# Three chained layers on one core: every low plane of the expert weights on VectorE, none on GpSimd

## The chip, the core and the metric

The kernel runs as one program on one core of a Trainium2 chip. A core has TensorE for matrix products, VectorE, ScalarE and GpSimd for work on tiles in on-chip memory, and SyncE, whose queue here issues most of the DMA transfers. In the profile these are PE (with PEld for the loading of weights), DVE, ACT, POOL and SP. The metric is the device time of one execution in microseconds (us). A difference is given against the kernel before.

## What is computed

Causal attention feeds a mixture of eight experts, in which every token goes to one expert, and that feeds a dense layer with `h - tanh(h)` between its two products. All inputs and outputs are float32.

```python
# attention: batch 4, 12 heads, 448 tokens, head size 64
scores = q @ k.T / 8, causal mask, softmax;  attn_out = attn @ v
x = attn_out as (1792, 768)
# experts: w1 is (8, 768, 1024), w2 is (8, 1024, 768)
logits = x @ w_gate;  e_idx = argmax(logits)
for e in range(8):
    mask = e_idx == e
    h = maximum(x[mask] @ w1[e], 0)
    out[mask] = gate_w * sigmoid(x @ w_output_gate)[e] * (h @ w2[e])
# dense layer: w_in is (768, 2048), w_out is (2048, 768)
h = x @ w_in;  return (h - tanh(h)) @ w_out
```

## The kernel before

Matrix products run in 16 bits. To keep accuracy, each operand is split into two float16 planes: a **high plane**, the value scaled by `WS` and rounded, and a **low plane**, the scaled value minus the high plane. A product takes three passes: high by high, high by low and low by high.

The program has three stages. In the expert stage the tokens of one expert are worked on in **slots** of 128. `slot()` first multiplies with w1 in two halves (72 matmuls each, tile `ph`); after each half `slot_relu` makes the high plane `hh` on ScalarE and the low plane `hl` on VectorE. Then it multiplies with w2 (tile `py`) in two column halves; each reads `hh` and `hl` block by block, the first four blocks from the first half of w1's product, the last four from the second. In between, TensorE transposes the rows of the next slot, and ScalarE and VectorE copy these out (tiles `xT`, `xT_n`, line 150 and 152). Every expert runs its first slot always, and further ones (`extra`, line 871) only if it has enough tokens: a branch on a count, which every engine takes for itself. With the data of the runs, experts 0, 3 and 5 run no further slot, experts 1, 4 and 7 run one, expert 2 two and expert 6 four. Expert 0's first slot in this stage is its second 128 tokens. The further slots also convert pieces of the dense layer's weights (`conv`: tiles `cu`, `cc`, `co`, stored to `wb_d`).

In the first slot of expert e the weights of expert e+1 are split. A **piece** is one block of 128 rows of w1 (128x1024, six of them) or of w2 (128x768, eight of them). `PLAN` lists the pieces in four groups. Each entry says which weight, which block, which engine makes the high plane (`scaled`, lines 112, 114 or 116), and which the low one (`rest_of`, line 120 on VectorE, lines 114 and 128 on GpSimd, where it takes a scaling into the scratch tile `scm` and a subtraction, in parts of 512 columns at most). Group by group, `fill_hi` and `fill_lo` are called at fixed places in `slot()`: the low planes of group 0 stand on their engine's queue between the two `hl` of the slot, those of groups 1 and 2 among the copies of transposed rows, those of group 3 at the end. After the low planes of a group, SyncE issues the loads of the same blocks of expert e+2 (`load_raw`, line 104): each waits until the piece in `raw1` or `raw2` has been read. Behind the last of them SyncE stores the slot's result (line 857), and then comes the branch at line 871. With expert 1, VectorE also makes the tables for the tokens' order (`order_a`, lines 1031 and 1039) ahead of group 3, and TensorE multiplies them (tile `order`, line 1058) before expert 1's further slot.

GpSimd's own queue also issues the gathers of token rows (`slot_rows`, line 801), which stay.

Of the kernel before, what the change touches and what calls it, by code (L numbers as in the profile page):

```python
# [26 lines left out]
E, F1 = 8, 1024  # L27
# [29 lines left out]
def build(ctx: ExitStack, tc: tile.TileContext, kq0, kq, v, wg, wo, w1, w2, wf, out):  # L57
# [45 lines left out]
    def load_raw(e, x, k, n=1):  # L103
        nc.sync.dma_start(out=(raw1, raw2)[x][:, k : k + n, :], in_=(w1, w2)[x][e, :, k : k + n, :])

    def w_tiles(e, zs=(0, 1)):
        return [w16s[e % 2][z].tile((([128, 2, KD, F1]), [128, 2, KF1, DM])[z], F16, tag=f"w{z + 1}", name=f"w{z + 1}_{e}")
                for z in zs]
# [9 lines left out]
    def rest_of(eng, out, in_, hi):  # L118
        if eng == "v":
            nc.vector.scalar_tensor_tensor(out=out, in0=in_, scalar=WS, in1=hi, op0=ALU.mult, op1=ALU.subtract)  # L120
        else:
            w = in_.shape[-1]
            h = scr[0].shape[-1]
            for o in range(0, w, h):
                c = slice(o, min(o + h, w))
                t = scr[0][:, 0 : c.stop - o]
                scaled("p", t, in_[:, c])
                nc.gpsimd.tensor_tensor(out=out[:, c], in0=t, in1=hi[:, c], op=ALU.subtract)  # L128

    def pieces_hi(w, plan):  # L130
        for x, k, eh, el in plan:
            scaled(eh, w[x][:, 0, k, :], (raw1, raw2)[x][:, k, :])

    def pieces(w, plan, nxt=None, hi=True):
        if hi:
            pieces_hi(w, plan)
        for x, k, eh, el in plan:
            rest_of(el, w[x][:, 1, k, :], (raw1, raw2)[x][:, k, :], w[x][:, 0, k, :])
        if nxt is not None and nxt < E:
            for x, k, eh, el in plan:  # L140
                load_raw(nxt, x, k)
# [751 lines left out]
    def conv_load(dst, r, eng=nc.sync):  # L893
        eng.dma_start(out=dst.rearrange("p n t -> p (n t)").unsqueeze(1), in_=wf32[:, ds(r, 1), :])
# [15 lines left out]
    def conv_fill(e, i):  # L910
# [4 lines left out]
        def fill(z):  # L915
# [10 lines left out]
    wi = [t.rearrange("p a b -> p (a b)").bitcast(F16).rearrange("p (c k f) -> p c k f", c=4, k=KD)  # L926
          for t in (raw1, raw2)]
    wif = [t.rearrange("p c k f -> p (c k f)") for t in wi]
    PLANS = {0: [[(1, 2 * z, "a", "p"), (1, 2 * z + 1, "a", "v")] for z in range(4)],
# [4 lines left out]
    PLAN = (  # L934
# [4 lines left out]
    )  # L939
    tpool = [mp_t]  # L940
    first = {}
    NI = 12
# [16 lines left out]
    def prep0(g, i, r0=None):  # L959
        bk = GS[g] + i  # L960
        src = ys_d[bk * 128 : (bk + 1) * 128] if r0 is None else ys_d[ds(r0, 128)]
        nc.sync.dma_start(out=yg_of(g, i), in_=src)
# [67 lines left out]
    def order_a(z):  # L1030
        eq = lambda t, pos, h, n: nc.vector.tensor_tensor(
            out=t, in0=pos.unsqueeze(2).to_broadcast([CP, h, n]), in1=io[:CP, 0:n].unsqueeze(1).to_broadcast([CP, h, n]),
            op=ALU.is_equal)
        if z < 2:
            cs = slice(z * NC_ // 2, (z + 1) * NC_ // 2)
            eq(oba[:, cs], pb[:, 0, cs], NC_ // 2, 128)
        else:
            eq(obm, pb[:, 1], NC_, NBLK)
            nc.vector.tensor_tensor(out=obb, in0=obm.unsqueeze(3).to_broadcast([CP, NC_, NBLK, 5]),
                                    in1=pcs.unsqueeze(2).to_broadcast([CP, NC_, NBLK, 5]), op=ALU.mult)  # L1040
# [23 lines left out]
    wts = {0: wts0, 1: wts1 + w_tiles(1, (1,))}  # L1064
# [14 lines left out]
    for e in range(E):  # L1079
# [7 lines left out]
        if e + 1 < E:  # L1087
            if e:
                wts[e + 1] = w_tiles(e + 1)

            def fill_hi(z, e=e):
                plan = PLANS.get(e, PLAN)
                todo = (plan[0][:2], plan[0][2:])[z] if z < 2 else plan[z - 1]
                pieces_hi(wts[e + 1], todo)

            def fill_lo(z, e=e):
                if e == 0 and z >= 2:
                    next(tl, None)
                pieces(wts[e + 1], PLANS.get(e, PLAN)[z], e + 2, False)
                if e == 1 and z > 1:  # L1100
                    order_a(z) if z < 3 else order_b()

            fill = (fill_hi, fill_lo)
        else:
            wo_ = [w16s[0][z].tile([128, KF2, DM], F16, tag=tg, name=f"wo_{z}") for z, tg in enumerate(("w1", "w2"))]
            wof = [t.rearrange("p k f -> p (k f)") for t in wo_]
            stg = [wof[0][:, z * 4096 : (z + 1) * 4096].bitcast(U32).rearrange("p (n t) -> p n t", t=2) for z in range(2)]
            stg += [wof[1][:, z * 2048 : (z + 1) * 2048] for z in range(2)]
            tot = nc.values_load(flg[0:1, 1:2], min_val=0, max_val=3 * MAXI)
            remaining(NDY - 2)  # L1110
            first["yg"] = [wof[1][:, z * 2 * DM : (z + 1) * 2 * DM].bitcast(F32) for z in range(3)]
            at_ = (wof[1][:, 6 * DM :], wof[0])
            first["yq"] = [[t[:, z * 2 * DM : (z + 1) * 2 * DM].rearrange("p (k x n) -> p k x n", k=KD, x=2)
                            for z in range(3)] for t in at_]
            first["dg"] = [[t[:, 6 * DM + 256 * z : 6 * DM + 256 * (z + 1)].bitcast(BF16).rearrange(
                "p (a n) -> p a n", a=2) for z in range(3)] for t in at_]
            first["sc"] = [t[:, 6 * DM + 768 : 6 * DM + 832].bitcast(F32) for t in at_]
            second = nc.values_load(flg[0:1, 0:1], engines=(SP,), min_val=0, max_val=128)
            for i in range(GB[0]):
                prep0(0, i, second * i if i else 0)  # L1120

            def fill(z):
                if z == 2:
                    for q in range(2):
                        conv_load(stg[q], NDY + q, nc.gpsimd)
                if z in (1, 2):
                    conv(cu[z - 1], co[z - 1][:, 0], co[z - 1][:, 1], "p")
                    conv_store(z - 1, nc.values_load(flg[0:1, z + 1 : z + 2], engines=(SP,), min_val=0, max_val=NDY - 1))
                if z == 3:
                    first_prep()  # L1130
# [241 lines left out]
```

## Time and profile before

| | before |
|---|---|
| time of three runs | 1077.86 us median (1073.29 to 1078.04) |
| the profiled execution: its time, its span | 1075.26 us, 1073.5 us |
| TensorE's granted clock, mean | 0.986 of full speed |
| attention stage | 0 to about 260 us |
| expert stage, experts 0 to 6 whose first slots split weights | 260 to about 490 us (expert 6's further slots to 549 us) |
| expert 7, then the dense layer | from 549 us |

The span runs from the first to the last instruction of the program; the execution's time lies 1.8 us above it. A row of the timeline gives a start and a length, and in square brackets how long the engine had been idle just before and what released it. A row that merges several instructions (x2, x3) gives the time from the first's start to the last's end. VectorE's instructions overlap a little, so that the next one starts up to 0.1 us before the one ahead has ended.

### The profile page before, as it was taken

Reading aid. Unit: us, or ns where it says so; the run is one execution under the profiler, and the core shown is the slowest. Engines: PE = TensorE matmul, PEld = TensorE weight load, DVE = VectorE, ACT = ScalarE, POOL = GpSimd, SP = SyncE. Lnnn points to the kernel's source line nnn. Section 1 sums busy time; section 2 is a strip of 40 time slices with the busy share of each in tenths; the row PEclk is TensorE's granted clock in tenths of the full one; section 3 lists DMA queues with packets and bytes.
Section 4 is the critical chain, followed back from the end, with each engine's and each line's share of the span. In section 5 each row is a group of like instructions: output and inputs, shape, how many; then the busy total and the mean of one; then the engine's idle time right before and its main releaser. Section 6 shows DMA issues by size and latency. Waiting matters only on the chain. (4 is left out here: it accounts for less than half of the span.)

```text
span 1073.5 us, 24251 instructions
## 1 busy us (share of the span) xinstructions
PE 994.7 (93%) x9186; PEld 748.5 (70%) x9186; DVE 821.6 (77%) x1579; ACT 592.8 (55%) x1190; POOL 607.5 (57%) x623
## 2 busy tenths in 40 slices
PE   5999999998989989888978877999999999999996
PEld 4999998996767767577866544666666666667763
DVE  7678888776877778779867799988788788786540
ACT  4686876774635355463323477766555556565430
POOL 5476766684877279686136778655543444443321
PEclk9999999998999999999999999999999999999999
DMA  8899997735888988885985705000001000000000
GB/s 248 220 268 298 259 252 196 215 103 165 297 314 314 322 278 292 313 297 183 339 313 202 287 11 211 16 31 30 15 24 45 15 24 16 15 16 15 16 23 23
DMA packets 62834, 174.94 MB, mean 163 GB/s; under 512 B 8400, under 2 KB 23376, under 8 KB 59584
## 3 DMA queue, kind: packets, MB, share of 16 engines
q1 hardware_dynamic: 56352, 147.20, 41.6%
q0 software_dynamic: 6304, 25.63, 8.3%
q8 instruction: 80, 1.31, 0.5%
q14 instruction: 98, 0.80, 0.2%
HBM read 133.09 MB, written 29.62 MB: 152 GB/s over the span
## 5 line engine op out<-in xcount | busy, mean ns | idle before, releaser
L1261 PE MATMUL fo<-wo,g 128*128 128x384 f16 x1344 | 228.2, 326 | 0.0
L1210 PEld LDWEIGHTS <-raw 128*128 128x128 f16 x1440 | 141.3, 98 | 96.2 <-issue 17.9
L1261 PEld LDWEIGHTS <-g 128*128 128x128 f16 x1344 | 131.2, 98 | 83.8
L1220 POOL TENSOR_TENSOR V<-cu,cc 128x384 f32<-128x384 f32 (+1 forms) x80 | 77.1, 963 | 198.5 <-ACT cu L1219 198.3
L161 PEld LDWEIGHTS <-w 128*128 128x128 f16 x2592 | 150.1, 100 | 13.4 <-issue 12.3
L1210 PE MATMUL fh<-cu,raw 128*128 128x384 f16 (+1 forms) x864 | 133.5, 310 | 12.4 <-DVE cc L1218 12.2
L173 PE MATMUL py<-w,hh 128*128 128x384 f16 x544 | 133.8, 328 | 9.3 <-ACT hh L168 9.2
L347 ACT ACTIVATE P<-s,nb 112x112 f32<-112x112 f32 (+1 forms) x192 | 90.0, 496 | 57.0 <-DVE rs L398 28.9
L384 PE MATMUL o<-v,PT 112*112 112x65 f32 x960 | 114.7, 259 | 0.0
L384 PEld LDWEIGHTS o<-v,PT 112*112 112x112 f32 x960 | 105.5, 178 | 0.2 <-ACT xt L406 0.2
L120 DVE SCALAR_TENSOR_TENSOR w<-raw,w 128x768 f16<-128x768 f32 (+1 forms) x70 | 97.6, 1439 | 9.3 <-ACT w L112 9.3
L173 PE MATMUL py<-w,hl 128*128 128x384 f16 x272 | 89.4, 329 | 11.4 <-DVE hl L169 11.4
L1238 DVE TENSOR_TENSOR V<-V,co 128x384 f32<-128x384 f32 (+1 forms) x80 | 99.9, 1249 | 0.0
L1219 ACT ACTIVATE cu<-cc 128x384 f32<-128x384 f32 (+1 forms) x80 | 40.1, 502 | 102.6 <-DVE cc L1218 102.6
L112 ACT ACTIVATE w<-raw 128x768 f16<-128x768 f32 (+2 forms) x101 | 84.3, 895 | 21.7 <-ACTq L871 9.6
L1223 POOL TENSOR_TENSOR X<-cc,X 128x384 f32<-128x384 f32 (+1 forms) x80 | 91.1, 1139 | 4.1 <-ACT X L1222 0.5
L1218 DVE TENSOR_TENSOR cc<-fh,co 128x384 f32<-128x384 f32 (+1 forms) x80 | 42.0, 525 | 65.5 <-PE fh L1210 53.6
L128 POOL TENSOR_TENSOR w<-scm,w 128x512 f16<-128x512 f32 (+1 forms) x58 | 81.4, 1403 | 11.5 <-issue 6.2
L333 DVE TENSOR_REDUCE nm<-s 112x2 f32<-112x224 f32 (+1 forms) x144 | 77.2, 536 | 13.0 <-PE s L325 11.4
L1230 DVE SCALAR_TENSOR_TENSOR V<-cu,V 128x384 f32<-128x384 f32 (+1 forms) x80 | 86.8, 1085 | 0.1
L173 PEld LDWEIGHTS <-hh 128*128 128x128 f16 x544 | 52.2, 98 | 42.0 <-ACT hh L168 10.5
L161 PE MATMUL ph<-xT_n,w 128*128 128x128 f16 x1152 | 69.3, 224 | 8.8 <-issue 2.5
(430 smaller groups left out, 2030.9 us busy)
## 6 DMA issues: line engine op xcount, KB each, us to landing
raw<-w SPq DMA_DIRECT2D x48, 512.0 KB
raw<-w SPq DMA_DIRECT2D x60, 384.0 KB
cu<-wf SPq DMA_DIRECT2D x22, 1024.0 KB
wb_d<-co SPq DMA_DIRECT2D x22, 512.0 KB
raw<-kq SPq DMA_DIRECT2D x11, 896.0 KB
ys_d<-yo SPq DMA_DIRECT2D x17, 384.0 KB
raw<-wb_d SPq DMA_DIRECT2D x8, 768.0 KB
xs_d<-xq SPq DMA_DIRECT2D x24, 224.0 KB
```

The source lines that it names most:

```text
L112: nc.scalar.activation(out=out, in_=in_, func=AF.Copy, scale=WS)
L120: nc.vector.scalar_tensor_tensor(out=out, in0=in_, scalar=WS, in1=hi, op0=ALU.mult, op1=ALU.subtract)
L128: nc.gpsimd.tensor_tensor(out=out[:, c], in0=t, in1=hi[:, c], op=ALU.subtract)
L161: nc.tensor.matmul(out=ph[:, (f % 4) * 128 : (f % 4 + 1) * 128], lhsT=w[0][:, ww, k, f * 128 : (f + 1) * 128], rhs=xTs[tag][:, xx, k, :], ...
L173: nc.tensor.matmul(out=py[:, 0:384], lhsT=hx[:, k, :], rhs=w[1][:, ww, k, z * 384 : (z + 1) * 384], start=(k == 0 and n == 0), stop=(k == ...
L347: nc.scalar.activation(out=d["P"][:, j, OFF[i] : OFF[i] + n], in_=d["s", m][:, z, :], func=AF.Exp, bias=d["nb"][:, 2 * i + j : 2 * i + j + ...
L384: nc.tensor.matmul(out=po[:, i, :], lhsT=d["PT"][:, g, o : o + CP], rhs=d["t"][3][:, hl, j, :], start=(j == 0), stop=(j == i))
L1210: nc.tensor.matmul(out=ph[:, 0:nt], lhsT=wi[ww][:, f // 4, k, f % 4 * 128 : (f % 4 + 1) * 128], rhs=yy[:, k, 0:nt], start=(q == 0), stop=( ...
L1223: nc.gpsimd.tensor_tensor(out=d["X"], in0=d["h"], in1=d["X"], op=ALU.subtract)
L1230: nc.vector.scalar_tensor_tensor(out=d["V"], in0=d[f"S{z}"], scalar=QD[z - 1], in1=d["V"], op0=ALU.add, op1=ALU.mult)
L1238: nc.vector.tensor_tensor(out=d["V"], in0=d["V"], in1=G[g % 2]["rs"][:, 1, 0:nt], op=ALU.mult)
L1261: nc.tensor.matmul(out=po[:, 0:384], lhsT=t[:, x, k, i * 128 : (i + 1) * 128], rhs=wo_[ww][:, k, z * 384 : (z + 1) * 384], start=(k == 0 a ...
```

## The change

The two special plans shrink to one, and no entry names GpSimd (`"p"`) any more. Low planes are all made by VectorE (`"v"`); high planes by ScalarE (`"a"`), but for block 0 of w2, which VectorE makes. Expert 1's own plan is gone: its filling uses the common one. The lines behind it move up by three.

```diff
-    PLANS = {0: [[(1, 2 * z, "a", "p"), (1, 2 * z + 1, "a", "v")] for z in range(4)],
-             1: ([(0, 2, "a", "p"), (0, 0, "a", "v"), (0, 1, "a", "v")],
-                 [(0, 5, "p", "p"), (0, 3, "a", "v"), (0, 4, "a", "v")],
-                 [(1, 2, "a", "p"), (1, 0, "a", "v"), (1, 1, "a", "v")],
-                 [(1, 5, "a", "p"), (1, 3, "a", "p"), (1, 4, "a", "v"), (1, 6, "a", "v"), (1, 7, "a", "v")])}
     PLAN = (
-        [(0, 2, "a", "p"), (0, 0, "a", "v"), (0, 1, "a", "v")],
-        [(0, 5, "p", "p"), (0, 3, "a", "v"), (0, 4, "a", "v")],
-        [(1, 2, "a", "p"), (1, 0, "v", "v"), (1, 1, "a", "v")],
-        [(1, 5, "a", "p"), (1, 3, "a", "v"), (1, 4, "a", "v"), (1, 6, "a", "v"), (1, 7, "a", "v")],
+        [(0, 2, "a"), (0, 0, "a"), (0, 1, "a")],
+        [(0, 5, "a"), (0, 3, "a"), (0, 4, "a")],
+        [(1, 2, "a"), (1, 0, "v"), (1, 1, "a")],
+        [(1, 5, "a"), (1, 3, "a"), (1, 4, "a"), (1, 6, "a"), (1, 7, "a")],
     )
+    PLANS = {0: [[(1, 2 * z, "a"), (1, 2 * z + 1, "a")] for z in range(4)]}
+    PLANS = {e: [[(*p, "v") for p in q] for q in PLANS.get(e, PLAN)] for e in range(E)}
...
-                plan = PLANS.get(e, PLAN)
+                plan = PLANS[e]
...
-                pieces(wts[e + 1], PLANS.get(e, PLAN)[z], e + 2, False)
+                pieces(wts[e + 1], PLANS[e][z], e + 2, False)
```

VectorE's queue in the first slot of expert 3, which splits the weights of expert 4 (`w_4`; `raw_89` is w1's staging tile, `raw_90` w2's). Before:

```order
L169 SCALAR_TENSOR_TENSOR hl_0_16895<-ph_0_0_16899,hh_0_16894 128x512
L120 SCALAR_TENSOR_TENSOR w_4_16877<-raw_89,w_4_16877 128x1024 x2
L169 SCALAR_TENSOR_TENSOR hl_0_16895<-ph_0_1_16984,hh_0_16894 128x512
L150 COPY xT_4488<-pt_I-17068_17069 128x768
L120 SCALAR_TENSOR_TENSOR w_4_16877<-raw_89,w_4_16877 128x1024 x2
L116 TENSOR_SCALAR w_4_16878<-raw_90 128x768
L150 COPY xT_n_85<-pt_I-17128_17129 128x768
L120 SCALAR_TENSOR_TENSOR w_4_16878<-raw_90,w_4_16878 128x768 x6
L871 COMPARE_AND_BRANCH
```

And in the changed kernel:

```order
L169 SCALAR_TENSOR_TENSOR hl_0_16856<-ph_0_0_16860,hh_0_16855 128x512
L120 SCALAR_TENSOR_TENSOR w_4_16838<-raw_89,w_4_16838 128x1024 x3
L169 SCALAR_TENSOR_TENSOR hl_0_16856<-ph_0_1_16942,hh_0_16855 128x512
L150 COPY xT_4488<-pt_I-17026_17027 128x768
L120 SCALAR_TENSOR_TENSOR w_4_16838<-raw_89,w_4_16838 128x1024 x3
L116 TENSOR_SCALAR w_4_16839<-raw_90 128x768
L150 COPY xT_n_85<-pt_I-17083_17084 128x768
L120 SCALAR_TENSOR_TENSOR w_4_16839<-raw_90,w_4_16839 128x768 x8
L871 COMPARE_AND_BRANCH
```

Between the two `hl` stand three pieces of w1 and not two, ahead of the copy of rows three and not two, and between `xT_n` and the branch eight pieces of w2 and not six. The same holds for experts 2 and 4 to 6.

GpSimd's queue at the same place, from the first piece to the first of w2. Before:

```order
L114 TENSOR_SCALAR scm<-raw_89 128x512
L128 TENSOR_TENSOR w_4_16877<-scm,w_4_16877 128x512
L114 TENSOR_SCALAR scm<-raw_89 128x512
L128 TENSOR_TENSOR w_4_16877<-scm,w_4_16877 128x512
L801 DMA xg_4485<-xs_d,idx 128x1536
L114 TENSOR_SCALAR w_4_16877<-raw_89 128x1024
L114 TENSOR_SCALAR scm<-raw_89 128x512
L128 TENSOR_TENSOR w_4_16877<-scm,w_4_16877 128x512
L114 TENSOR_SCALAR scm<-raw_89 128x512
L128 TENSOR_TENSOR w_4_16877<-scm,w_4_16877 128x512
L801 DMA xg_n<-xs_d,idx 128x1536
L114 TENSOR_SCALAR scm<-raw_90 128x512
```

And in the changed kernel, from the gather ahead of that slot to the branch behind it:

```order
L801 DMA xg_4484<-xs_d,idx 128x1536
L865 REGISTER_ALU
L1365 BRANCH_PREFETCH_HINT
L801 DMA xg_4485<-xs_d,idx 128x1536
L801 DMA xg_n<-xs_d,idx 128x1536
L871 COMPARE_AND_BRANCH
```

Only the gathers are left (tiles `xg`): they follow one another with nothing between them.

VectorE's queue in the first slot of expert 1, around the tables that TensorE multiplies (`cc`). Before:

```order
L150 COPY xT_n_85<-pt_I-8532_8533 128x768
L120 SCALAR_TENSOR_TENSOR w_2_8282<-raw_90,w_2_8282 128x768 x2
L1031 TENSOR_TENSOR cc<-pb,io 112x224
L1039 TENSOR_TENSOR cc<-cc,pcs 112x1120
L120 SCALAR_TENSOR_TENSOR w_2_8282<-raw_90,w_2_8282 128x768 x3
L1061 TENSOR_REDUCE smt<-order 128x14
```

And in the changed kernel:

```order
L120 SCALAR_TENSOR_TENSOR w_2_8269<-raw_89,w_2_8269 128x1024 x3
L116 TENSOR_SCALAR w_2_8270<-raw_90 128x768
L150 COPY xT_n_85<-pt_I-8514_8515 128x768
L120 SCALAR_TENSOR_TENSOR w_2_8270<-raw_90,w_2_8270 128x768 x3
L1028 TENSOR_TENSOR cc<-pb,io 112x224
L1036 TENSOR_TENSOR cc<-cc,pcs 112x1120
L120 SCALAR_TENSOR_TENSOR w_2_8270<-raw_90,w_2_8270 128x768 x5
L1058 TENSOR_REDUCE smt<-order 128x14
```

One piece of w2 more, and a high plane at line 116, stand ahead of the two rows of the tables; two pieces more stand behind them.

## Rows read from the trace of the kernel before

**Rows 1.** One stretch: us, busy us (instructions), clock, DMA share, GB/s.

```profile
260.00:490.00 230.00, 206.33 (x2513) 165.79 (x2513) 176.67 (x234) 113.36 (x164) 162.60 (x144) 0.98 0.83 294
```

**Rows 2.** TensorE's waits, 260 to 490 us: total, times, longest.

```profile
PE py L173 <- DVE hl L169: 10.3, 9, 2.6
PE order L1058 <- DVE cc L1039: 2.9, 1, 2.9
...
PE ph L161 <- ACT xT_n L152: 1.0, 1, 1.0
```

**Rows 3.** TensorE's timeline: rows with a wait, experts 3 to 6.

```profile
391.37 0.34 PE L173 MATMUL py<-w,hl 128*128 128x384 f16 x1 [2.62 <-DVE hl L169]
...
426.33 0.34 PE L173 MATMUL py<-w,hl 128*128 128x384 f16 x1 [1.68 <-DVE hl L169]
...
446.50 0.50 PE L173 MATMUL py<-w,hh 128*128 128x384 f16 x2 [1.76 <-ACT hh L168]
...
467.59 0.51 PE L148 MATMUL pt_I-29923_29924<-identh,xg 128*128 128x128 f16 x6 [0.64 <-DVEq L871]
...
488.49 0.34 PE L173 MATMUL py<-w,hl 128*128 128x384 f16 x1 [1.06 <-DVE hl L169]
...
506.29 0.50 PE L173 MATMUL py<-w,hh 128*128 128x384 f16 x2 [1.44 <-ACT hh L168]
```

**Rows 4.** VectorE's groups by shape, 260 to 490 us: busy, mean ns, idle.

```profile
L120 DVE SCALAR_TENSOR_TENSOR w<-raw,w 128x768 f16<-128x768 f32 x39 | 50.1, 1337 | 7.0 <-ACT w L112 7.0
L120 DVE SCALAR_TENSOR_TENSOR w<-raw,w 128x1024 f16<-128x1024 f32 x25 | 40.9, 1673 | 0.5 <-ACT w L112 0.5
```

**Rows 5.** VectorE's timeline, end of the attention stage.

```profile
249.93 3.48 DVE L120 SCALAR_TENSOR_TENSOR w<-raw,w 128x1024 f16<-128x1024 f32 x3
```

**Rows 6.** GpSimd's timeline, same place.

```profile
250.21 4.11 POOL L717 DMA_INDIRECT x<-xs_d,idx  x1 [5.82 <-DVE cnt L719]
```

**Rows 7.** VectorE's groups, 416.1 to 416.9 us: one piece of w2.

```profile
L120 DVE SCALAR_TENSOR_TENSOR w<-raw,w 128x768 f16<-128x768 f32 x1 | 0.9, 944 | 0.0
```

**Rows 8.** GpSimd's groups by shape, 260 to 490 us: the two largest.

```profile
L128 POOL TENSOR_TENSOR w<-scm,w 128x512 f16<-128x512 f32 x40 | 63.8, 1595 | 10.0 <-issue 6.2 <-ACT w L112 0.7 <-POOL scm L114 0.2
L114 POOL TENSOR_SCALAR scm<-raw 128x512 f32<-128x512 f32 x40 | 35.5, 886 | 3.3 <-DMA raw<-w 1.2
```

**Rows 9.** VectorE's timeline, first slot of expert 3.

```profile
385.88 0.69 DVE L169 SCALAR_TENSOR_TENSOR hl<-ph,hh 128x512 f16<-128x512 f32 x1 [6.82 <-ACT hh L168]
386.49 4.22 DVE L120 SCALAR_TENSOR_TENSOR w<-raw,w 128x1024 f16<-128x1024 f32 x2
...
396.27 8.08 DVE L120 SCALAR_TENSOR_TENSOR w<-raw,w 128x768 f16<-128x768 f32 x6
```

**Rows 10.** ScalarE's groups by shape, 260 to 490 us: w1's high planes.

```profile
L112 ACT ACTIVATE w<-raw 128x1024 f16<-128x1024 f32 x30 | 30.4, 1054 | 18.0 <-ACTq L871 9.6 <-DMA wb_d<-co 5.0 <-PE ph L161 3.5
```

**Rows 11.** Waits of SyncE's queue, 260 to 490 us.

```profile
SPq L104 <- POOL scm L114: 54.7, 18, 6.0
SPq L871 <- SPq L871: 37.6, 14, 6.3
```

**Rows 12.** Timeline of SyncE's queue, behind expert 3's first slot.

```profile
409.82 0.13 SPq L857 DMA_DIRECT2D ys_d<-yo  x1
418.09 1.62 SPq L104 DMA_DIRECT2D raw<-w  x3
```

**Rows 13.** ScalarE's timeline: rows with a wait, experts 4 to 6.

```profile
417.83 0.49 ACT L832 ACTIVATE yo<-py 128x384 f32<-128x384 f32 x1 [6.82 <-SPq L871]
...
443.95 2.00 ACT L112 ACTIVATE w<-raw 128x1024 f16<-128x1024 f32 x2 [5.89 <-ACTq L871]
...
504.60 1.15 ACT L112 ACTIVATE co<-cc 128x512 f16<-128x512 f32 x2 [3.99 <-DMA wb_d<-co]
```

**Rows 14.** VectorE's timeline, first slot of expert 1.

```profile
288.70 0.69 DVE L169 SCALAR_TENSOR_TENSOR hl<-ph,hh 128x512 f16<-128x512 f32 x1 [0.80 <-DVEq L871]
...
300.92 1.54 DVE L1039 TENSOR_TENSOR cc<-cc,pcs 112x1120 bf16<-112x1120 bf16 x1
```

## The prediction

> **What bounds the kernel now.** I read the windows by stage first, because the change touches only the split of the expert weights. Between 260 and 490 us TensorE is busy for 206.33 of 230 us at a granted clock of 0.98, VectorE for 176.67, GpSimd for 162.60 and ScalarE for 113.36 [rows 1]. TensorE sets the pace, and all that this change can give or take is in the 23.7 us in which it is not busy. No engine is near its limit on average, so the question is which wait ends last at which place.
>
> TensorE's waits tell that. The largest is for `hl`, the low plane of the activations that VectorE makes: 10.3 us in 9 waits; then 2.9 us for the tables of the order [rows 2]. The timeline places them: 2.62 us in expert 3's first slot at 391.37, 1.68 in expert 4's further slot at 426.33, 1.06 in expert 6's at 488.49, and waits of 0.64 to 1.76 us for ScalarE's `hh` or for a branch at 446.50, 467.59 and 506.29 [rows 3]. So VectorE is the engine that TensorE waits for in the first slots, and the change gives VectorE more pieces. Whether that hurts hangs on what a piece costs once GpSimd is quiet.
>
> **The price of a piece.** In this stretch a low piece of w1 takes VectorE 1673 ns on average (25 of them, 40.9 us) and one of w2 1337 ns (39, 50.1 us) [rows 4]. At the end of the attention stage three pieces of w1 take 3.48 us together, 1.16 each [rows 5], while GpSimd has only a gather in hand [rows 6]. A piece of w2 in a stretch in which GpSimd doesn't compute takes 944 ns [rows 7]. So the same instruction is 1.4 times as long in the expert stage, where GpSimd splits: 63.8 us of subtractions and 35.5 of scalings in the two largest groups, and these leave [rows 8]. In expert 3's first slot two pieces of w1 took 4.22 us, 2.11 each [rows 9]. Only the gathers stay on GpSimd, and a gather doesn't lengthen the pieces beside it [rows 5, 6]. I take 1.16 and 0.94 us; the bounds are these and the means of rows 4, since nothing but GpSimd's silence speaks for the shorter price.
>
> VectorE's load then: with the 12 pieces of w1 and 17 of w2 that the plans give it in addition, 37 and 56, against 25 and 39. At the short price this is 37 x 1.16 + 56 x 0.944 = 95.8 us, against 40.9 + 50.1 = 91.0 now: 4.8 us more. At the long one it is 37 x 1.673 + 56 x 1.337 = 136.8, 46 us more. So VectorE takes over GpSimd's work almost for nothing, or becomes the late engine.
>
> **Part by part.**
>
> *Three pieces between the two `hl`.* In expert 3's slot the first `hl` starts at 385.88, the pieces 0.61 later, the second `hl` behind 4.22 us of pieces [rows 9]; TensorE goes on at 391.37 after waiting 2.62 [rows 3]. From the first `hl` on it had 391.37 - 385.88 - 2.62 = 2.87 us of other work. After: 0.61 + 3 x 1.16 + 0.61 = 4.7 us, which leaves a wait of 1.8: here 0.8 us is won although a piece was added. But it stands in every full plan now. Of the 10.3 us of rows 2, 1.68 and 1.06 are in further slots; 7.6 are in first slots. If five of the six slots of experts 1 to 6 wait 1.8 us, it is 9.0; this costs **+1.4 us**. The bounds are three slots (5.4, -2.2) and six (10.8, +3.2).
>
> *The tables of the order.* In expert 1's first slot VectorE's queue from the first `hl` at 288.70 to the end of the tables at 302.46 [rows 14] gets two pieces of w1, one low piece of w2 and one high plane more (the last taken at 0.94 too, an estimate), 2 x 1.16 + 2 x 0.94 = 4.2 us; the four pieces of w1 and two of w2 that already stand there get shorter by 4 x 0.51 + 2 x 0.39 = 2.8. TensorE waits for the end of it (2.9 us in rows 2), so **+1.4 us**. The bounds are 0 (those six pieces cost 2.11 before, as in expert 3's slot [rows 9], and win more) and +1.9 (their gain is a little smaller).
>
> *ScalarE.* Six more high planes of w1 at 1054 ns [rows 10], one of w2 less: 5.5 us on an engine that is idle for half of the stretch [rows 1]. Its cover is the product with w1, under which it has only `hh` to make. Cost 0; if a plane came ahead of a late `hh`, 1 us a slot.
>
> *SyncE's loads and its branch.* SyncE's queue waits 54.7 us in 18 waits for GpSimd to have read a staging tile [rows 11]. Those waits go. They hold the branch up too: behind expert 3's first slot SyncE issues the store at 409.82 and the next loads only at 418.09, after its jump [rows 12]; its own branch accounts for 37.6 us in 14 waits [rows 11]. ScalarE's `yo` of expert 4 waits 6.82 us for that jump [rows 13], a high plane comes late, VectorE's low piece after it, and TensorE waits 1.68 at 426.33 [rows 3]. With the last load of a slot no longer held by GpSimd, SyncE reaches the branch some 4 to 5 us earlier (the longest of the held loads waited 6.0, rows 11), and the jump lies under TensorE's product with w2. The waits at 426.33 and 488.49 vanish: **-2.7 us**, bounds 0 and -2.7.
>
> *Waits behind the other branches.* In expert 5 ScalarE's queue comes out of its branch after 5.89 us and then makes two planes [rows 13]; TensorE waits 1.76 for `hh` at 446.50. At 467.59 it waits 0.64 for VectorE's branch, and at 506.29 1.44 for `hh`, as ScalarE's `co` had waited 3.99 us for a store of a conversion [rows 3, 13]. VectorE's group 3 is eight pieces and not six, but 8 x 0.944 = 7.6 us against 8.08 [rows 9], so VectorE reaches its branch no later, ScalarE and the conversions are freed of the longer pieces ahead. I take off all three, 3.8, less 0.8 for what is left of the first: **-3.0 us**, bounds 0 and -3.8.
>
> The sum: 1.4 + 1.4 - 2.7 - 3.0 = -2.9 us, against the profiled execution's own 1075.26, which is 2.6 us below the median of the runs and 2 above the fastest. Stages behind 600 us are unchanged, so the gain is carried to the end. That is 1072.4; since early loads push every later load forward as well, and the terms have priced only waits that I could follow, I put **1072 us**. The likeliest case's own range is 1068 to 1076. Some 0.5%, 5.4 us, is what can be told from no change.
>
> **Rivals.**
>
> *The jumps stay where they are (no change).* SyncE's branch took 6.3 us at the longest and ScalarE's 5.89 [rows 11, 13], long beside any instruction here. If the jump lasts longer when more transfers are under way, then loads that are issued earlier lie in front of it, and the two terms of -2.7 and -3.0 go to 0. What is left is +2.8 us: 1078. For it speaks a DMA share of 0.83 [rows 1]; against it that the 14 waits of SyncE average 2.7 us, so many are short. The Trainium skill ("Runtime: NRT & Kernel Launch", section "Instruction fetch mechanics") says that a taken branch whose target lies outside of the pages already loaded forces a DMA fetch of the target before execution goes on; the trace agrees as far as the pause behind the branch goes, and no row shows where the fetch stands among the other transfers. By that rule the jump would keep its length whatever is done to the split, and the time would be that of this rival.
>
> *VectorE becomes the late engine (slower).* If the long price is not GpSimd's doing, but that of the DMA writes or of ScalarE reading the same staging tile, three pieces take 5.0 us between the two `hl`, and the wait is 0.61 + 5.02 + 0.61 - 2.87 = 3.4 us. Five of them are 17, +9.2 against 7.6 now; the tables come 2 x 1.67 + 2 x 1.34 = 6.0 us later; the gains are lost, as VectorE reaches its branch 8 x 1.337 = 10.7 instead of 8.08 us after the last copy. Together +15: 1090. It decides from about 1.4 us a piece of w1 on: there three pieces take the 4.22 us of the two in rows 9. Against it speak rows 5 and 7. A milder form (1.3 us a piece) gives 5 x 2.25 - 7.6 = +3.6 for the `hl`, +2 for the tables, and half the gains: 1078 to 1081.
>
> *More than I can follow (faster).* GpSimd's 54.7 us of held loads and its contention reach further than the waits priced: of TensorE's 23.7 us not busy only the rows named were counted. If nearly all waits for branches and `hh` behind them go, and the `hl` waits shrink as in expert 3 by 0.8 in place of growing, the sum is -2.7 - 3.8 - 3 = -9.5: 1066.
>
> **How the numbers follow.** The forecast's case has 0.42, the jumps that stay 0.16, VectorE late 0.18, the larger gain 0.24. Faster by over 0.5% is the larger gain and about two fifths of the forecast's case (whose middle lies near that mark): 0.42. Slower is VectorE late without the half of its milder form, and a little of the jumps: 0.17. Within 0.5% is the rest, 0.41. For the range I leave out the strong form of the late VectorE (about 0.1) and the outer end of the larger gain: 1063 to 1081.
>
> **What the profile after would show.** Right: no rows of w pieces on GpSimd between 260 and 490 us; VectorE's groups at about 1.16 and 0.94 us; waits of 1.8 us for `hl` in first slots, with TensorE's total for `hl` about 9; the wait for the tables near 4.3; no waits of SyncE's loads on GpSimd, its branch behind expert 3 at about 405; no wait at the places of 426.33, 488.49 and 506.29. Wrong: pieces above 1.4 us with GpSimd silent; jumps that end as late as now; a new wait of TensorE for ScalarE's `hh` behind a sixth high plane; or loads that start earlier and hold back the gathers.

## The result, and the profile after

The changed kernel takes 1064.61 us (median of 4 runs, 1061.27 to 1071.40) against 1077.10 of the kernel before; the ratio is 0.9892, with a 95% interval of 0.9846 to 0.9938. In a second set of eight runs it came out at 0.9898 (0.9863 to 0.9932). It is faster by 1.1%, some 12 us; the forecast was a gain of 3 to 6 us with a range down to 1063. The direction was right and the time lies in the range, but near its lower end: the gain is two to four times the one forecast.

The profiled execution is the slowest of the four, 1071.40 us. Its attention stage, which the change doesn't touch, took 10 us longer than in the trace of before: TensorE is busy there for 249.0 us at a mean granted clock of 0.97, and for 242.2 at 0.99 before. So expert 0's slot begins at 270.9 and not at 260.8 us, and times are to be read from the start of a slot. A stretch of 230 us of the stage again, against [rows 1] (stretch, busy us of TensorE, its weight loads, VectorE, ScalarE and GpSimd, granted clock, DMA share, GB/s):

```profile
270.00:500.00 230.00, 214.00 (x2652) 172.37 (x2653) 176.09 (x284) 121.25 (x176) 35.81 (x28) 0.99 0.85 308
```

GpSimd falls from 162.60 to 35.81 us, VectorE stays where it was, TensorE is busy for 214.00 us in place of 206.33, at a clock of 0.99 and not 0.98. It isn't the same work: the stretch now holds 2652 matmuls and not 2513. VectorE's groups in it, which answer to [rows 4]:

```profile
L120 DVE SCALAR_TENSOR_TENSOR w<-raw,w 128x768 f16<-128x768 f32 x56 | 49.5, 951 | 2.0 <-ACT w L112 2.0
L120 DVE SCALAR_TENSOR_TENSOR w<-raw,w 128x1024 f16<-128x1024 f32 x37 | 43.1, 1217 | 0.0
```

Seventeen and twelve pieces more, and 92.6 us busy in place of 91.0. The pieces stand at 0.95 and 1.22 us on average, at the short price; where neighbours overlap, the busy time counts them once, so that three in a row take 3.49 us, 1.16 each. Other work of VectorE got shorter too, such as its high planes of w2, before (first row) and after:

```profile
L116 DVE TENSOR_SCALAR w<-raw 128x768 f16<-128x768 f32 x5 | 6.5, 1292 | 0.0
```

```profile
L116 DVE TENSOR_SCALAR w<-raw 128x768 f16<-128x768 f32 x6 | 3.3, 553 | 0.0
```

GpSimd's rows for w are gone; the gathers are left:

```profile
L801 POOL DMA_INDIRECT xg<-xs_d,idx x20 | 25.5, 1273 | 161.7 <-issue 38.0 <-PE pt_I-30136_30137 L148 19.1 <-PE pt_I-8781_8782 L148 15.8
L801 POOL DMA_INDIRECT xg_n<-xs_d,idx x7 | 10.2, 1456 | 25.7 <-PE pt_I-25631_25632 L148 4.9 <-PE pt_I-17083_17084 L148 4.9 <-PE pt_I-21357_21358 L148 4.9
```

TensorE's waits in the stretch, against [rows 2]:

```profile
PE py L173 <- DVE hl L169: 7.1, 7, 1.9
PE ph L161 <- issue: 4.3, 3, 2.2
PE order L1055 <- DVE cc L1036: 2.3, 1, 2.3
PE ph L161 <- PEq L871: 2.1, 4, 0.7
...
PE py L173 <- ACT hh L168: 0.2, 1, 0.2
```

The total for `hl` went from 10.3 to 7.1 us, for the tables from 2.9 to 2.3, and for `hh` from 2.2 to 0.2. The waits above 1 us that are left for `hl` stand in the first slots of experts 3 to 6; the waits of [rows 3] in further slots, for `hh` and for VectorE's branch have no row any more:

```profile
394.48 0.34 PE L173 MATMUL py<-w,hl 128*128 128x384 f16 x1 [1.33 <-DVE hl L169]
...
413.93 0.34 PE L173 MATMUL py<-w,hl 128*128 128x384 f16 x1 [1.27 <-DVE hl L169]
...
450.65 0.34 PE L173 MATMUL py<-w,hl 128*128 128x384 f16 x1 [1.88 <-DVE hl L169]
...
471.50 0.34 PE L173 MATMUL py<-w,hl 128*128 128x384 f16 x1 [1.88 <-DVE hl L169]
```

Expert 3's slot shows how the wait of 1.33 us comes about (VectorE's timeline, against [rows 9]):

```profile
389.72 0.69 DVE L169 SCALAR_TENSOR_TENSOR hl<-ph,hh 128x512 f16<-128x512 f32 x1 [5.95 <-ACT hh L168]
390.33 3.49 DVE L120 SCALAR_TENSOR_TENSOR w<-raw,w 128x1024 f16<-128x1024 f32 x3
393.73 0.68 DVE L169 SCALAR_TENSOR_TENSOR hl<-ph,hh 128x512 f16<-128x512 f32 x1
```

Three pieces take 3.49 us where two took 4.22. No other first slot wins by it: in those of experts 1, 2, 4, 5 and 6 the two took 2.48 to 3.32 us before, and three take 3.48 or 3.49 now. The first `hl` itself is late: it waited 5.95 us for ScalarE's `hh`, and the reason for that is one row further back, in ScalarE's timeline:

```profile
389.09 0.60 ACT L168 ACTIVATE hh<-ph 128x512 f16<-128x512 f32 x1 [1.25 <-DVEq L871]
```

`hh` was held by VectorE's own branch behind the slot before. So what is left of this wait is a piece too many and a jump that ends late.

SyncE's queue behind expert 3's first slot, against [rows 12], and ScalarE's `yo` that waits for it, against [rows 13]:

```profile
408.21 0.28 SPq L857 DMA_DIRECT2D ys_d<-yo  x1
419.25 2.08 SPq L104 DMA_DIRECT2D raw<-w  x4
```

```profile
418.99 0.49 ACT L832 ACTIVATE yo<-py 128x384 f32<-128x384 f32 x1 [3.42 <-SPq L871]
```

The store stands 6.7 us behind the start of expert 4's slot (401.5) in place of 11.7 (409.82 less 398.1), the jump still takes 5.7 us (6.3 before), and `yo` waits 3.42 us and not 6.82. Behind the jump SyncE's queue stands still again, and its waits there come to 9.9 us in all, where they were 7.2. So `yo` goes on 17.5 us behind the slot's start in place of 19.7: of the 5.0 us won at the store, 2.2 are left. SyncE's waits for GpSimd [rows 11] have gone; its waits for VectorE's pieces went from 11.9 to 24.5 us:

```profile
SPq L871 <- SPq L871: 41.6, 14, 5.7
SPq L104 <- DVE w L120: 24.5, 35, 4.3
```

### The profile page after: what moved, and what is told of

It reads as the page before. It is cut to its first block, busy times and chain, and to the rows that moved or that the text cites. A ratio compares the mean times of both kernels' runs of the same rounds, so it can differ in the third digit from the quotient of the medians.

```text
span 1069.7 us, 24122 instructions
## 1 busy us (share of the span) xinstructions
PE 996.5 (93%) x9186; PEld 750.8 (70%) x9186; DVE 811.7 (76%) x1609; ACT 597.8 (56%) x1195; POOL 475.0 (44%) x501
## 3 DMA queue, kind: packets, MB, share of 16 engines
q8 instruction: 80, 1.31, 0.5%
## 5 line engine op out<-in xcount | busy, mean ns | idle before, releaser
L161 PEld LDWEIGHTS <-w 128*128 128x128 f16 x2592 | 147.4, 99 | 14.2 <-issue 13.1
L384 PE MATMUL o<-v,PT 112*112 112x65 f32 x960 | 118.0, 264 | 0.0
L384 PEld LDWEIGHTS o<-v,PT 112*112 112x112 f32 x960 | 109.0, 183 | 0.1
L801 POOL DMA_INDIRECT xg<-xs_d,idx x24 | 29.5, 1230 | 168.3 <-issue 38.4
L112 ACT ACTIVATE w<-raw 128x768 f16<-128x768 f32 (+2 forms) x106 | 89.1, 904 | 23.2 <-ACTq L871 15.6
L333 DVE TENSOR_REDUCE nm<-s 112x2 f32<-112x224 f32 (+1 forms) x144 | 77.3, 537 | 17.3 <-PE s L325 16.0
L161 PE MATMUL ph<-xT,w 128*128 128x128 f16 x1296 | 75.4, 221 | 0.0
```

The costliest lines, as they stand in the source:

```text
L112: nc.scalar.activation(out=out, in_=in_, func=AF.Copy, scale=WS)
L161: nc.tensor.matmul(out=ph[:, (f % 4) * 128 : (f % 4 + 1) * 128], lhsT=w[0][:, ww, k, f * 128 : (f + 1) * 128], rhs=xTs[tag][:, xx, k, :], ...
L333: nc.vector.tensor_reduce(out=nm[:, c0:c1], in_=d["s", m], op=ALU.max, axis=AX.X, negate=True)
L384: nc.tensor.matmul(out=po[:, i, :], lhsT=d["PT"][:, g, o : o + CP], rhs=d["t"][3][:, hl, j, :], start=(j == 0), stop=(j == i))
```

## The experiments

One stretch is compared in all of them: from the first product of expert 0's slot to that of expert 7's, in which every kernel runs the same 3160 matmuls. "Idle" is the stretch less TensorE's busy time, from one row of the windows view each.

| kernel | median us | ratio to before (95%) | stretch | TensorE busy | idle |
|---|---|---|---|---|---|
| before | 1077.1 | | 289.4 | 262.7 | 26.7 |
| before, second trace | 1076.56 (one run) | | 290.3 | 265.1 | 25.2 |
| changed | 1064.61 | 0.9892 (0.9846 to 0.9938) | 276.1 | 258.5 | 17.7 |
| changed, second trace | 1063.62 | 0.9898 (0.9863 to 0.9932) | 274.2 | 258.0 | 16.3 |
| noise2 | 1096.48 | 1.0183 (1.0163 to 1.0203) | 308.7 | 271.6 | 37.1 |
| w1_back | 1065.85 | 0.9907 (0.9877 to 0.9937) | 276.4 | 259.7 | 16.6 |
| w2_back | 1071.76 | 0.9959 (0.9934 to 0.9983) | 288.0 | 264.2 | 23.7 |
| hold | 1067.42 | 0.9911 (0.9892 to 0.9929) | 277.2 | 258.4 | 18.8 |
| hold2 | 1081.57 | 1.0027 (1.0006 to 1.0049) | 296.5 | 264.3 | 32.1 |
| hi_back | 1068.46 | 0.9922 (0.9894 to 0.9950) | 278.9 | 257.1 | 21.7 |
| two_between | 1062.48 | 0.9868 (0.9846 to 0.9891) | 275.0 | 258.5 | 16.5 |
| two_tables | 1059.19 | 0.9841 (0.9817 to 0.9865) | 273.1 | 257.7 | 15.4 |

Each ratio is against runs of the kernel before in the same set; the median of these was 1077.1, 1076.0, 1077.05 and 1078.87 us in the four sets. So kernels of different sets are compared by their ratios here.

The windows view's rows behind the stretch, before and changed:

```profile
260.84:550.20 289.36, 262.70 (x3160) 209.25 (x3161) 227.87 (x322) 133.43 (x201) 182.69 (x164) 0.98 0.84 295
```

```profile
270.86:546.97 276.11, 258.45 (x3160) 206.54 (x3161) 213.38 (x349) 137.94 (x206) 48.84 (x42) 0.99 0.86 308
```

For the same work VectorE is busy for 14.5 us less, although it makes 29 pieces more: much of what it does beside them got shorter.

The trace of w2_back is of the slowest of its 12 runs, 1082.78 us; its stretch is long for that reason too, and only its waits are read.

**Both kernels once more.** No edit.

> The changed kernel once more, for more runs beside the kernel before and a second trace. If the gain is in the expert stage's waits, TensorE's stretch from expert 0's slot to expert 7's takes 276 us again (289 before) and the ratio lies between 0.985 and 0.995. If part of it was a lucky clock, the ratio comes out at 0.995 or above and the stretch at 280 us or more.

> The kernel before once more, for a second trace of it. If the stretch from expert 0's slot to expert 7's is a property of the kernel, it takes 286 to 291 us again (289.4 in the first trace; 276.1 and 274.2 in the two of the changed kernel), and the waits for hl are in the same slots. If the first trace was a bad draw, it comes out near 282 us or less.

Both held: 290.3 and 274.2 us. So the difference of the stretch is 13 to 16 us and belongs to the kernels. Some waits move between executions: expert 3's for `hl`, 2.62 us in the first trace of before, is 0.45 in the second, expert 4's first slot has one of 0.81, and expert 6's further slot has 2.25 in place of 1.06. The sum is steadier than its terms.

**Contention: noise2.** It computes all planes as the changed kernel does, and in addition work that nobody reads.

```diff
+    GP = {(0, 2), (0, 5), (1, 2), (1, 5)}
+    nc.gpsimd.memset(scr[0], 0.0)
+    def noise(e, z):
+        for x, k, eh, el in PLANS[e][z]:
+            if (x, k) in GP if e else k % 2 == 0:
...
+                    nc.gpsimd.tensor_scalar(out=t, in0=t, scalar1=1.0, scalar2=1.0, op0=ALU.mult, op1=ALU.mult)
+                    nc.gpsimd.tensor_tensor(out=t, in0=t, in1=wts[e + 1][x][:, 0, k, c], op=ALU.subtract)
...
                 pieces(wts[e + 1], PLANS[e][z], e + 2, False)
+                noise(e, z)
```

> The changed kernel, with useless work on GpSimd at the places of its former low planes: per half piece a multiplication of the scratch tile by one in place, and the subtraction of the weights' high plane from it, into itself. Nothing waits for the result, the staging tile isn't read and no load is held. Theory (contention: GpSimd's computing lengthens VectorE's pieces): w1 pieces back at 1.5 to 1.7 us, w2 at 1.2 to 1.35; three long pieces between the two hl, so waits of 2 to 3 us for hl in several first slots; time 8 to 20 us above the changed kernel (1072 to 1084). Rival (held loads: the gain came from SyncE's loads no longer waiting for GpSimd): within 3 us of the changed kernel, about 1064.

```profile
L120 DVE SCALAR_TENSOR_TENSOR w<-raw,w 128x768 f16<-128x768 f32 x48 | 59.9, 1310 | 0.0
L120 DVE SCALAR_TENSOR_TENSOR w<-raw,w 128x1024 f16<-128x1024 f32 x37 | 54.4, 1521 | 0.5 <-ACT w L112 0.5
```

```profile
PE py L173 <- DVE hl L169: 18.5, 12, 3.3
PE order L1068 <- DVE cc L1049: 6.5, 1, 6.5
```

```profile
SPq L104 <- DVE w L120: 77.3, 60, 7.4
```

The pieces are back at 1.52 and 1.31 us, and VectorE's high planes of w2 at 0.87, though nothing waits for what GpSimd computes, and no load is held by it; TensorE waits for no gather there either. The time is some 31 us above the changed kernel, more than the 8 to 20 of the theory. The rival (held loads alone) is out. This comes near the late VectorE of the prediction: with the long price the change would have ended at about 1096, where the prediction worked out 1090. It hurts in one slot above all: expert 1's takes 29.7 us (20.3 in the changed kernel), 6.5 of it the wait for the tables. The waits in the further slots of experts 4 and 6 come back too, about 1 us each, and SyncE's loads are held by VectorE for 77.3 us.

**Where it counts: w1_back, w2_back.** Two edits of one line, each of which gives GpSimd a part of its low planes back.

```diff
+    GP = {(0, 2), (0, 5)}
-    PLANS = {e: [[(*p, "v") for p in q] for q in PLANS.get(e, PLAN)] for e in range(E)}
+    PLANS = {e: [[(*p, "p" if e and p[:2] in GP else "v") for p in q] for q in PLANS.get(e, PLAN)] for e in range(E)}
```

```diff
+    GP = {(1, 2), (1, 5)}
-    PLANS = {e: [[(*p, "v") for p in q] for q in PLANS.get(e, PLAN)] for e in range(E)}
+    PLANS = {e: [[(*p, "p" if (p[:2] in GP if e else p[1] % 2 == 0) else "v") for p in q] for q in PLANS.get(e, PLAN)]
+             for e in range(E)}
```

> The changed kernel, with the low planes of blocks 2 and 5 of w1 made by GpSimd again (12 pieces), all of w2 left on VectorE. Theory (contention, places apart): two long pieces between the two hl (about 2 us each), waits of 1.7 to 2.6 us for hl in first slots as before, but none at the further slots of experts 4 and 6, where only w2's group matters; 3 to 6 us above the changed kernel (about 1069). Rival (held loads of w1 count as well): the branch of SyncE comes late again and the waits in the further slots return too, 8 us or more.

> The changed kernel, with the low planes of blocks 2 and 5 of w2 (and of expert 0's even blocks) made by GpSimd again, all of w1 left on VectorE. Theory: the first slots' hl waits stay as in the changed kernel (1.3 to 1.9 us in experts 3 to 6), the waits in the further slots of experts 4 and 6 come back (1 to 1.7 us each), with the later branch of expert 5; 4 to 7 us above the changed kernel (about 1070). Rival (only what lies between the two hl counts): within 2 us of the changed kernel.

w1_back is 1 to 2 us above the changed kernel, inside both of its intervals, where 3 to 6 were expected. The two pieces between the two `hl` aren't 2 us each: the pair takes 2.35 to 3.31 us in the six slots, less than three short ones. In expert 3's slot it takes 2.35, and GpSimd computes beside it at the two edges only (a subtraction ends at 383.44 and the next scaling begins at 385.52; the pair runs from 383.38 to 385.73). So its `hl` waits are fewer, not longer, and one of them, 0.97 us, is in expert 6's further slot, both of which the theory had wrong; its wait for the tables is longer:

```profile
PE order L1056 <- DVE cc L1037: 4.1, 1, 4.1
PE py L173 <- DVE hl L169: 3.6, 4, 1.7
```

w2_back gives back 7 us, as the theory said, but only in part by the waits that it named. Of the two in further slots, that of expert 6 is there for `hl`, and at the place of expert 4's stand 0.45 us:

```profile
496.59 0.34 PE L173 MATMUL py<-w,hl 128*128 128x384 f16 x1 [0.80 <-DVE hl L169]
```

A wait of 1.85 us for `hl` in expert 1's first slot, which nobody expected, is back as well (1.72 in the kernel before, none in the changed one), and the tables are waited for 3.27 us in place of 2.34. With the other half moved, w2's planes are worth about 7 us and w1's 1 to 2.

**ScalarE's sixth plane: hi_back.** One entry.

```diff
-        [(0, 5, "a"), (0, 3, "a"), (0, 4, "a")],
+        [(0, 5, "p"), (0, 3, "a"), (0, 4, "a")],
```

> The changed kernel, with the high plane of block 5 of w1 on GpSimd again, as before (six instructions of about 1.07 us), in place of ScalarE. If ScalarE's six planes cost nothing, as the prediction's sum has it, the time is that of the changed kernel within 2 us; a gain of 1 to 3 us here would show that they did cost. Rival: even 6 us of GpSimd's computing lengthen VectorE's pieces beside it, by up to 1 us a slot: 1 to 4 us slower.

The rival won in the trace: the `hl` waits grow by 0.6 to 1.3 us in each of experts 3 to 6, to 10.6 us in 6. The time is some 3 us above the changed kernel, with intervals that overlap. Expert 3's slot shows why in two rows, one of GpSimd and one of VectorE:

```profile
385.08 1.19 POOL L114 TENSOR_SCALAR w<-raw 128x1024 f16<-128x1024 f32 x1
```

```profile
383.02 4.33 DVE L120 SCALAR_TENSOR_TENSOR w<-raw,w 128x1024 f16<-128x1024 f32 x3
```

One GpSimd instruction of 1.19 us lies in the time of the three pieces, and they take 4.33 us in place of 3.49. The Trainium skill ("SBUF — State Buffer", section "SBUF: two separate sides") has a VectorE instruction with two inputs in SBUF (the on-chip memory) and a GpSimd instruction that reads SBUF take turns at a shared port pair, which the one that starts first holds for its whole length. The 0.84 us lost here, less than the 1.19 us of that instruction, doesn't speak against that.

**SyncE's held loads: hold, hold2.** In both, the last load of a first slot waits for GpSimd, which computes next to nothing. hold2 adds ten copies of one column.

```diff
+                if e and z == 3:
+                    pieces(wts[e + 1], PLANS[e][z], None, False)
...
+                    nc.gpsimd.dma_start(out=nz[:, 0:1], in_=wts[e + 1][1][:, 1, 7, 0:1])
+                    nc.gpsimd.tensor_copy(out=nz[:, 1:2], in_=nz[:, 0:1])
+                    for _ in range(10):
+                        nc.gpsimd.tensor_copy(out=nz[:, 1:2], in_=nz[:, 0:1])
+                    nc.gpsimd.tensor_copy(out=nf[:, 0:1], in_=raw2[:, 7, 0:1])
...
+                        load_raw(e + 2, 1, 7)
```

> The changed kernel, with the last load of a first slot (block 7 of w2) held by GpSimd as loads were before, but without GpSimd computing: behind VectorE's last piece GpSimd moves one column by a small DMA, copies it, and copies one column of the staging tile, on which the load waits. Pieces stay short. Theory of the late branch: SyncE reaches its branch some 3 to 5 us later behind the first slots, ScalarE's yo of expert 4's further slot waits for the jump as before, and the waits for hl in the further slots of experts 4 and 6 (1.7 and 1.1 us) come back; 2 to 4 us above the changed kernel. Rival (contention alone): those waits came from long pieces, so they don't return, and the time stays within 1.5 us.

> As hold, with ten more copies of one column on GpSimd ahead of the one that the load waits for: in hold SyncE's jump behind expert 3's first slot ended 16.5 us after the next slot's start (18.2 in the kernel before, 12.8 and 11.3 in the changed one). If a late jump of SyncE alone makes the wait for hl in expert 4's further slot, 3 us more bring it back (1 to 2 us there), and the time rises another 1 to 3 us above hold. If that wait needs long pieces too, it stays away.

hold is some 2 us above the changed kernel, inside both of its intervals, and the two waits did not come back. But it didn't test them: SyncE's jump began late, yet took only 2.8 us, and `yo` went on 17.1 us behind the start of expert 4's slot, as in the changed kernel (17.5 and 15.5). In hold2 it waited 9.65 us for SyncE and went on at 23.9 us, later than in the kernel before (19.7 and 21.0), and TensorE waits in expert 4's further slot with all pieces short:

```profile
420.78 0.49 ACT L832 ACTIVATE yo<-py 128x384 f32<-128x384 f32 x1 [9.65 <-SPq L871]
```

```profile
426.55 0.50 PE L173 MATMUL py<-w,hh 128*128 128x384 f16 x2 [1.98 <-ACT hh L168]
427.83 0.34 PE L173 MATMUL py<-w,hl 128*128 128x384 f16 x1 [0.77 <-DVE hl L169]
```

So a late jump makes this wait with short pieces too, from a lateness of `yo` on that lies between 17.5 us and hold2's 23.9; the kernel before lies between them. hold2 overshoots, and its 1081.57 us also hold a wait of 2.90 us for a gather that GpSimd issued late, so it doesn't price the held loads of the kernel before. noise2 shows the same wait with long pieces and no load held by GpSimd. How much each had of the 1.68 us in the kernel before stays open.

**The third piece: two_between, two_tables.** The first moves block 1 of w1 into the next group, the second also puts the tables ahead of three pieces.

```diff
-        [(0, 2, "a"), (0, 0, "a"), (0, 1, "a")],
-        [(0, 5, "a"), (0, 3, "a"), (0, 4, "a")],
+        [(0, 2, "a"), (0, 0, "a")],
+        [(0, 1, "a"), (0, 5, "a"), (0, 3, "a"), (0, 4, "a")],
```

```diff
+                if e == 1 and z == 2:
+                    order_a(z)
                 pieces(wts[e + 1], PLANS[e][z], e + 2, False)
-                if e == 1 and z > 1:
-                    order_a(z) if z < 3 else order_b()
+                if e == 1 and z == 3:
+                    order_b()
```

> The changed kernel, with two pieces of w1 between the two hl and four in the next group. If the remaining wait for hl in first slots (1.3 to 1.9 us in four slots) comes from the third piece, each wait falls by the 1.14 us of a piece, the total for hl from 5 to 7 us to about 1 to 2, and the time is 3 to 5 us below the changed kernel (about 1060). Rival: the four pieces ahead of the copies of the transposed rows make a wait of their own for xT, and the time stays within 1.5 us.

> As two_between, and in expert 1's slot VectorE makes the tables of the order ahead of the three pieces of w2 and not behind them. The wait for the tables (2.3 us) ends 2.6 us earlier, that is, goes to 0: 2.3 us below two_between, 5 to 7 below the changed kernel. Rival: the pieces of w2 then come late for the next slot's loads, and the gain shows up as a wait in expert 1's further slot or expert 2's first.

```profile
PE py L173 <- DVE hl L169: 4.0, 7, 0.8
PE ph L161 <- issue: 3.9, 2, 2.2
PE order L1055 <- DVE cc L1036: 3.1, 1, 3.1
```

```profile
PE ph L161 <- issue: 4.5, 3, 2.2
PE pt_I-29843_29844 L148 <- DVEq L871: 2.4, 1, 2.4
PE py L173 <- DVE hl L169: 1.8, 4, 0.8
```

In two_between the wait of expert 3 falls from 1.33 to 0.44, of expert 5 from 1.88 to 0.81, of expert 6 from 1.88 to 0.74, and expert 4's goes: about the 1.14 us of a piece each, as expected; but the total for `hl` is 4.0 us and not 1 to 2, as waits of 0.81 and 0.78 us stand in expert 0's slot and in expert 6's further one. The tables come 0.8 us later for it. By its ratio it gains some 3 us, inside both intervals of the changed kernel, where 3 to 5 were expected, and its stretch of 275.0 us lies between the two of the changed kernel, so this gain isn't shown. With the tables first, their wait is gone, and 1059.19 us is the lowest median of all, some 6 us below the changed kernel by the ratio, as expected; its interval (to 0.9865) still touches the changed kernel's (from 0.9846, and 0.9863 in the second set). New waits have taken part of it back, such as 2.4 us for VectorE's branch in expert 6's slot.

## Why the prediction came out as it did

The point of the forecast, 1072, is missed by 7 us. That the time lies in the range is owed to its lower end, which the rival of the larger gain gave. In the sum, the two terms that were added cost next to nothing or less, one of those taken off was too small, and the clock was left out.

**The price of a piece: right.** 0.95 and 1.22 us against the forecast 0.94 and 1.16, and the pieces keep VectorE busy for 1.6 us more than before where 4.8 were reckoned. The short price was the choice on which all hung; noise2 shows that it is GpSimd's silence that gives it, not the place of the pieces. What the prediction didn't see is that the rest of VectorE's work gets shorter with them.

**Three pieces between the two `hl`: next to nothing, where the sum has +1.4.** The wait of 1.8 us per slot was sized well (1.33, 1.27, 1.88 and 1.88 in the first trace), but "five of the six slots" was not: experts 1 and 2 don't wait. Expert 1's first `hl` starts 5.8 us behind its slot's start (295.77 less 289.97) and not 7.7 as in expert 3's (389.72 less 381.99): VectorE stands only 0.80 us behind its branch there, and three pieces then end in time. In expert 2's slot the first `hl` starts 7.4 us behind the slot's start, but TensorE itself had stood 1.69 us in its first product. In all the wait for `hl` went from 10.3 and 9.0 us in the two traces of before to 7.1 and 5.1. Of that, 2.7 and 4.0 us stood in further slots and are gone; the first slots have 7.6 and 5.0 before, and 7.1 and 5.1 after.

**The tables: the sign was wrong.** Forecast +1.4 and a wait near 4.3; measured 2.34 and 2.33 in the two traces, 0.5 less than the 2.86 of both traces of before. VectorE's way from the first `hl` to the end of the tables takes 13.8 us as before. The first instruction of the tables before, and then the whole way after:

```profile
299.48 1.34 DVE L1031 TENSOR_TENSOR cc<-pb,io 112x224 bf16<-112x224 f32 x1
```

```profile
295.77 0.69 DVE L169 SCALAR_TENSOR_TENSOR hl<-ph,hh 128x512 f16<-128x512 f32 x1 [0.80 <-DVEq L871]
296.38 3.49 DVE L120 SCALAR_TENSOR_TENSOR w<-raw,w 128x1024 f16<-128x1024 f32 x3
...
304.25 0.55 DVE L116 TENSOR_SCALAR w<-raw 128x768 f16<-128x768 f32 x1
...
307.79 0.39 DVE L1028 TENSOR_TENSOR cc<-pb,io 112x224 bf16<-112x224 f32 x1
308.28 1.32 DVE L1036 TENSOR_TENSOR cc<-cc,pcs 112x1120 bf16<-112x1120 bf16 x1
```

The four added instructions are paid for by more than the six pieces: the two instructions of the tables fell from 1.34 to 0.39 and from 1.54 [rows 14] to 1.32 us, and the high plane took 0.55 and not the 0.94 estimated. The result is a little beyond the lower bound, 0, for which the prediction gave another reason (that the six pieces cost 2.11 us each before; those of w1 took 1.47 to 1.66 here).

**ScalarE at nothing: not contradicted.** TensorE's waits for a high plane from ScalarE did not grow: none in the first trace after and 0.4 us in the second, 0.4 and 0.8 before. hi_back shows that the alternative costs 0.6 to 1.3 us in each of four slots, by VectorE; it doesn't measure ScalarE by itself.

**SyncE's branch: right in place and effect.** -2.7 us forecast, and both waits are gone in both traces; the store stands 6.7 us behind the slot's start, as forecast (405 less 398.1, 6.9). The reason given (loads held by GpSimd) isn't the only one possible: hold2 makes such a wait without long pieces, noise2 without loads held by GpSimd.

**The waits behind other branches: right in kind, a little too small.** The three waits of 1.76, 0.64 and 1.44 us are gone, with 0.72 us more in expert 5; 0.3 and 0.8 us for `hh` stand in expert 6's third further slot, where the second trace of before has 1.72. Some -4.0 where the sum has -3.0. ScalarE's jump in expert 5 is still 5 us long:

```profile
437.23 1.14 ACT L112 ACTIVATE co<-cc 128x512 f16<-128x512 f32 x2
443.38 2.00 ACT L112 ACTIVATE w<-raw 128x1024 f16<-128x1024 f32 x2 [5.00 <-ACTq L871]
```

The conversions ahead of it end 0.9 us behind the start of the slot's first product (438.37 against 437.43) and not 3.4, and ScalarE goes on 3.4 us earlier against TensorE's work. Thus the rival "the jumps stay where they are" had the length about right and the consequence wrong: SyncE's queue spends 41.6 us in 14 waits of its own behind the branch after, and 37.6 before, but the jump's start moved, and that was enough. The Trainium skill ("Runtime: NRT & Kernel Launch", section "Instruction fetch mechanics") says that a taken branch whose target isn't among the pages already loaded must wait for a fetch by DMA; these pauses agree with that, and no row shows the fetch itself.

**What the sum left out: the clock.** Idle time fell by 9 us (25.9 on average of two traces to 17.0), against 2.9 in the sum; the terms above make some 8 of them. Another 5.7 us is TensorE's busy time for the same matmuls, 263.9 to 258.2 on average, which the prediction held constant. The slot of expert 2 shows it, before (first row) and after:

```profile
321.65:342.89 21.24, 18.96 (x216) 15.75 (x217) 13.88 (x15) 13.59 (x19) 13.31 (x11) 0.92 0.81 309
```

```profile
329.13:348.17 19.04, 17.34 (x216) 14.13 (x217) 13.22 (x17) 13.41 (x19) 3.81 (x3) 1.00 0.73 258
```

216 matmuls take 18.96 us at a granted clock of 0.92, and 17.34 at 1.00. The second traces agree (18.96 at 0.92, 17.51 at 1.00). Before, TensorE had stood 2.27 and 2.21 us inside this slot's first product, and after 1.69 and 1.75. That the shorter waits kept the clock up is argued from such slots, and from noise2 and hold2 below; no run changes a wait alone. 8.9 and 5.7 make 14.6 us in the stretch, and expert 7's slot is 1.3 us longer on average after (24.8 and 25.3, from 24.3 and 23.3). From the start of expert 0's slot to the program's end the traces take 812.7 and 812.3 us before, and 798.8 and 797.6 after: 14 us. The medians are 12 apart, with an interval from 7 to 17. The rival "more than I can follow" had the size, 1066, without this cause.

## What to carry to other kernels

Price an instruction by the stretch in which its neighbour is silent, not by its mean in the loaded one: here 29 pieces more cost VectorE 1.6 us, as GpSimd's work had been in the price of the others, and the rest of VectorE's work got shorter too. Before taking one slot as the model of all, read the same rows in the others: expert 3's pair of pieces was the longest of six. Waits can cost more than their own length where TensorE's granted clock is lower behind them, so compare the busy time of the same matmuls, not only the waits. When a new order leaves a wait, look one releaser further back: it was a branch on the engine behind the one that the row names.

## What the runs showed of the hardware

- The granted clock goes with TensorE's waits over a stretch. In noise2 it is 0.85 to 0.93 in the slots of experts 1, 2, 4, 5 and 6, and the same 3160 matmuls take 271.6 us against 258. In hold2 expert 3's slot, with waits of 1.20 and 1.73 us, has 0.93. It isn't a rule for one slot: expert 0's shows 1.00 in one trace of the changed kernel and 0.89 in the other, and the longer wait ahead of it (2.23 against 1.39 us) in the trace with 1.00. Each figure is a mean over a slot of the two levels, 2.4 and 1.2 GHz.
- SyncE's jump behind expert 3's first slot took 6.3 us in the kernel before, 5.7 and 5.4 in the traces of the changed one, 2.8 in hold and 2.7 in hold2, and ScalarE's `yo` waited for the queue to come out of it (1.60 to 9.65 us). What made the short ones short wasn't settled.
- VectorE's instructions on w took longer while GpSimd computed: 1.67 and 1.34 us for a piece in the kernel before, 1.52 and 1.31 in noise2, 1.22 and 0.95 with GpSimd silent; 1.29, 0.87 and 0.55 for the high plane of w2 at line 116.
